# One core's decode attention beside an MLP: which engine issues the loads, and each load marked as one packet

## The chip, the core and the metric

The kernel runs on one of the eight cores of a Trainium2 chip. The core has TensorE (PE, matrix products), VectorE (DVE), ScalarE (ACT), GpSimd (POOL) and SyncE (SP), which work side by side and wait for one another by semaphores, and 16 DMA engines that move data between the memory (HBM) and the core's own SBUF. The metric is the time of one execution on the device in microseconds, as the median of several runs; shorter is better.

## The reference

One token's row `x` (512 numbers, bf16) goes through two branches, which a sigmoid gate mixes:

```python
g = sigmoid((x * gate_w).sum(-1))
q = (x @ wq).reshape(32 heads, 128)
a = concat_h(softmax(q_h @ k_cache_h.T * 128**-0.5) @ v_cache_h) @ wo
b = (silu(x @ w_gate) * (x @ w_up)) @ w_down
return g * a + (1 - g) * b
```

Each of the 32 heads has 65,536 cached keys and as many values of 128 numbers: 16.8 MB of K and as much V a head, some 1,074 MB in all. `wq` and `wo` are 4.2 MB each, `w_gate`, `w_up` and `w_down` 1.8 MB each. Every byte is used once.

## The kernel before

One SBUF tensor `mem` of 184 blocks of 1 KB per partition holds everything that is loaded. K and V of a head come in halves (`z` = 0 and 1), each 8.4 MB, 64 KB on each of the 128 partitions. K half 0 goes to block `KA` = 32, V half 0 to `VA` = 120 and V half 1 to `VZ` = 96; K half 1 goes to `KZ` = 0, except for head 0, where it goes to `V0` = 96, the place of `wq`. So the K halves of the next head may be loaded only when those of this one have been used, and likewise V.

**Start.** SyncE issues the weights (lines 211 to 213): `wq` to block 96, `w_gate` to 0, `w_up` to 14, `w_down` to 160. Then it issues K half 0 of head 0 in two pieces of 32 KB per partition, counted on `ka0` and `ka1` (225). ACT issues the rows `x` and `gate_w` (214, 215). PE computes q from `wq` (460, then `s_q`), lays it out (466), computes gate and up products (488), and with DVE's results in `guT` the down product (496, then `s_b`). GpSimd waits for `s_q` before it loads K half 1 of head 0 over `wq` (236, 237).

**A head.** DVE turns each K half by eight transposes of 32x32 blocks from `mem` into `kt` (lines 326 for head 0, 419 and 426 for the rest; `ktdone` counts them, 16 a head). PE takes each transposed piece and makes scores of it in the bank `psS` (476, `qkdone`). DVE then finds the maximum (340, 342), with PE's help for the step across partitions (551, 553); ACT takes the exponentials into `pa` (292); DVE shuffles them to `pb` (335); and PE multiplies them with V (529) in four parts, 40 and 24 matmuls for half 0 and 40 and 24 for half 1 (`pvdone` counts them, from 4). PE's values of a head run between the scores of the next: half 0 after six pieces of its first K half, half 1 after its second.

**Who issues what, and when.** From line 236 GpSimd issues all K and V, with a wait before each load for the place that it overwrites: K half 0 of head 1 at `ktdone` 8, V half 0 of head 0 at `ktdone` 13 and `s_b`, K half 1 of head 1 at `ktdone` 20, V half 1 of head 0 at `pvdone` 5; then a loop over the heads with the same four loads (247 to 255). At the end it issues `wo` without its last rows (257), the last head's V in eight pieces of falling size (`tail`, 264), and the rest of `wo` (266, 267). Each load has a semaphore that its landing raises by 16; K half 0 of heads 1 to 31 counts on `ka`, and line 411 waits for `16 i` in head `i`. ACT and SyncE store the result (306 and 228).

**End.** The last head's second half is multiplied piece by piece as the `tail` loads land (565), then mixed with the rest (604), copied (304) and stored.

Of the kernel before, what the change touches and what calls it, by code (L numbers as in the profile page):

```python
# [21 lines left out]
def bass_gated_mix__mha_block_cached__swiglu_ffn__decode_kernel(  # L22
# [11 lines left out]
    out: bass.AP,  # L34
):
    _, H, S, Dh = A_k_cache.shape
    D = A_wq.shape[0]
    F = B_w_gate.shape[1]
# [3 lines left out]
    HR = R // 2  # L42
# [6 lines left out]
    KA, KZ, VA, VZ, V0 = 32, 0, 120, 96, 96  # L49
# [13 lines left out]
    WOJ, WO31 = V0, V0 + 1  # L63

    with ExitStack() as ctx:
        def sb(name, shape, dt, align=32):
            return ctx.enter_context(nc.sbuf_tensor(name, shape, dt, align_bytes=align))
# [4 lines left out]
        def sem(name):  # L72
            return ctx.enter_context(nc.semaphore(name))
# [33 lines left out]
        fin = sb("fin", [P, 128], BF16)  # L107

        def at(kb, n):
            return mem[:, kb * KB:kb * KB + n]  # L110
# [7 lines left out]
        mrow, amx, Lt = psM[0:1, 0:128], psM[:, 256:257], psM[:, 257:258]  # L118
        gm = sc[0:1, 5:6]

        names = ("x", "gw", "wq", "wg", "wu", "wd", "ka0", "ka1", "ka", "kz", "va", "vz", "wo", "wj", "w31")
        d = {n: sem("d_" + n) for n in names}
        dt_ = [sem(f"d_t{i}") for i in range(len(tail))]
        s_ones = sem("s_ones")
# [50 lines left out]
        s_fin = sem("s_fin")  # L175
        s_zz = sem("s_zz")
        s_out2 = sem("s_out2")
# [3 lines left out]
        out_dram = out.rearrange("a b (c n) -> (a b c) n", c=4)  # L181
        gw_dram = gate_w.rearrange("(a d) -> a d", a=1)
        w_dram = {
            "wq": A_wq.rearrange("(p c) n -> p (c n)", c=Dc),
            "wg": B_w_gate.rearrange("(p c) f -> p (c f)", c=Dc),
            "wu": B_w_up.rearrange("(p c) f -> p (c f)", c=Dc),
            "wd": B_w_down.rearrange("(p c) n -> p (c n)", c=FC),
            "wo": A_wo.rearrange("(p j) n -> p (j n)", p=P),
        }
        wj_dram = w_dram["wo"][:, 31 * D:32 * D]  # L190
        w31_dram = A_wo.rearrange("(h d) n -> h d n", d=Dh)[H - 1]
        WQ, WG, WU, WD, WO = V0, 0, 14, V0 + 64, 64
# [8 lines left out]
        def place(kind, h, z):  # L201
            if kind == "k":
                return (KA, V0)[z] if isinstance(h, int) and h == 0 else (KA, KZ)[z]
            return (VA, VZ)[z]

        def kv_dram(cache, h):
            if isinstance(h, int):
                return cache[0, h].rearrange("(b p r) d -> b p (r d)", b=2, p=P)
            return cache[0, ds(h, 1)].rearrange("a (b p r) d -> b (a p) (r d)", b=2, p=P)

        for n, kb in (("wq", WQ), ("wg", WG), ("wu", WU), ("wd", WD)):
            src = w_dram[n]
            nc.sync.dma_start(at(kb, src.shape[1]), src).then_inc(d[n], 16)
        nc.scalar.dma_start(xrow[0:1, :], xr_dram).then_inc(d["x"], 16)
        nc.scalar.dma_start(gwrow[0:1, :], gw_dram).then_inc(d["gw"], 16)
        ctx.callback(lambda: nc.scalar.wait_ge(s_out, 16))
        ctx.callback(lambda: nc.sync.wait_ge(s_out2, 16))
        block = ctx.enter_context(nc.Block())

        half = HR // 2 * Dh  # L220

        @block.sync
        def _(sp):
            for n in range(2):
                sp.dma_start(at(KA + 32 * n, half), kv_dram(A_k_cache, 0)[0][:, n * half:n * half + half]).then_inc(
                    (d["ka0"], d["ka1"])[n], 16)
            sp.wait_ge(s_fin, 1)
            sp.dma_start(out_dram[2:4, :], fin[32:34, :]).then_inc(s_out2, 16)

        @block.gpsimd  # L230
        def _(pool):
            def load(kind, h, z):
                cache = A_k_cache if kind == "k" else A_v_cache
                pool.dma_start(at(place(kind, h, z), HR * Dh), kv_dram(cache, h)[z]).then_inc(d[kind + "az"[z]], 16)  # L234

            pool.wait_ge(s_q, 1)
            load("k", 0, 1)
            pool.wait_ge(ktdone, NP)
            load("k", 1, 0)
            pool.wait_ge(ktdone, 2 * NP - 3)  # L240
            pool.wait_ge(s_b, 1)
            load("v", 0, 0)
            pool.wait_ge(ktdone, 2 * NP + NP // 2)
            load("k", 1, 1)
            pool.wait_ge(pvdone, 5)
            load("v", 0, 1)
            with nc.gpsimd.Fori(0, H - 2) as i:  # L247
                pool.wait_ge(ktdone, i * (2 * NP) + (4 * NP - 4))
                load("k", i + 2, 0)
                pool.wait_ge(pvdone, i * 4 + 7)  # L250
                load("v", i + 1, 0)
                pool.wait_ge(ktdone, i * (2 * NP) + (4 * NP + NP // 2))  # L252
                load("k", i + 2, 1)
                pool.wait_ge(pvdone, i * 4 + 9)
                load("v", i + 1, 1)
            pool.wait_ge(ktdone, 2 * NP * H - NP)
            pool.dma_start(at(WO, 31 * D), w_dram["wo"][:, 0:31 * D]).then_inc(d["wo"], 16)
            src = A_v_cache[0, H - 1].rearrange("(b p r) d -> b p (r d)", b=2, p=P)
            need = {0: (ktdone, 2 * NP * H - 4), 1: (ktdone, 2 * NP * H), 2: (pvdone, 4 * H - 1)}
            for n, (kb, r0, nr) in enumerate(tail):  # L260
                if n in need:
                    pool.wait_ge(*need[n])
                b, o = divmod(r0, HR)
                pool.dma_start(at(kb, nr * Dh), src[b][:, o * Dh:(o + nr) * Dh]).then_inc(dt_[n], 16)  # L264
            pool.wait_ge(pvdone, 4 * H)
            pool.dma_start(at(WOJ, D), wj_dram).then_inc(d["wj"], 16)
            pool.dma_start(at(WO31, D), w31_dram).then_inc(d["w31"], 16)

        @block.scalar
        def _(act):  # L270
# [38 lines left out]
        def _(dve):  # L309
# [7 lines left out]
            def transposes(z):  # L317
                dve.wait_ge(d[("ka0", "kz")[z]], 16)
                for c, u in enumerate(k_order[z]):
                    i = NP * z + c  # L320
                    if i == NP // 2:
                        dve.wait_ge(d["ka1"], 16)
                    if i >= 2:
                        dve.wait_ge(qkdone, i - 1)
                    src = at(place("k", 0, z) + 8 * u, PR * Dh).bitcast(U32)
                    nc.vector.transpose(kt[:, i % 2, :].rearrange("p (j r t) -> p r j t", j=2, t=32),  # L326
                                        src.rearrange("p (r j t) -> p r j t", j=2, t=32)).then_inc(ktdone, 1)

            def shuffle(z, s):
                c0 = 256 * z  # L330
                for g in range(4):
                    for b in range(4):
                        dst = pb[32 * g:32 * g + 32, c0:c0 + 256].rearrange("p (n b) -> p n b", b=4)[:, :, b]
                        sr = pa[32 * b:32 * b + 32, c0:c0 + 256].rearrange("p (n g) -> p n g", g=4)[:, :, g]
                        last = nc.vector.tensor_copy(dst, sr)  # L335
                last.then_inc(s, 1)
# [7 lines left out]
            def late(pv, sl, so):  # L344
                dve.wait_ge(pvdone, pv)
                shuffle(1, s_pbz)
                dve.wait_ge(s_L, sl)
                dve.wait_ge(s_or, so)
                nc.vector.reciprocal(Li, Lt).then_inc(s_li, 1)
# [57 lines left out]
            with nc.vector.Fori(1, H) as i:  # L407
                n = i * (2 * NP)
                v = i * 4
                dma = i * 16  # L410
                dve.wait_ge(d["ka"], dma)
                for c, u in enumerate(k_order[0]):
                    if c == NP // 2:
                        dve.wait_ge(expdone, i)
                        dve.wait_ge(pvdone, v - 2)
                        shuffle(0, s_pba)
                    dve.wait_ge(qkdone, n + (c - 1))  # L417
                    src = at(KA + 8 * u, PR * Dh).bitcast(U32)
                    nc.vector.transpose(kt[:, c % 2, :].rearrange("p (j r t) -> p r j t", j=2, t=32),  # L419
                                        src.rearrange("p (r j t) -> p r j t", j=2, t=32)).then_inc(ktdone, 1)  # L420
                late(v, i, i)
                dve.wait_ge(d["kz"], dma + 16)
                for c, u in enumerate(k_order[1]):
                    dve.wait_ge(qkdone, n + (NP + c - 1))
                    src = at(KZ + 8 * u, PR * Dh).bitcast(U32)
                    nc.vector.transpose(kt[:, c % 2, :].rearrange("p (j r t) -> p r j t", j=2, t=32),  # L426
                                        src.rearrange("p (r j t) -> p r j t", j=2, t=32)).then_inc(ktdone, 1)
                top(i, n + 2 * NP)
# [206 lines left out]
```

## Time and profile before

| | |
|---|---|
| median of 3 runs | 2527.52 us (2527.16 to 2527.83) |
| profiled execution, its time | 2528.12 us |
| its span, first to last instruction | 2526.7 us |
| busy: PE, DVE, ACT, POOL | 1708.3, 1412.3, 64.7, 73.3 us |
| moved by DMA | 1087.93 MB, 431 GB/s over the span |
| queue 0 (GpSimd's loads) | 19,232 packets, 1069.69 MB |
| queue 1 (SyncE's) | 868 packets, 18.09 MB |
| granted TensorE clock, mean | 0.722 |

The view of DMA issues gives for each kind of load its median time from issue to landing: 29.1 us for the three V tail loads of 4 MB, 12.3 for `wq`, 16.0, 23.3 and 44.3 for the three MLP weights, 58.0 for the two K pieces that SyncE issues.

How to read it: "busy" adds up an engine's own instructions. A row of a timeline gives start, length, engine, source line, operation, output and input; in brackets stand the idle time before it and what ended it. The engine name with a q (SPq, POOLq) is its sequencer, which issues DMAs. In a row of windows stand the stretch, its length, the busy time of PE, PEld (weight loading), DVE, ACT and POOL with the number of instructions, the granted clock, the mean share in which the 16 DMA engines were busy, and GB/s. A row of a DMA queue gives its kind, packets, MB and the time of its packets as a share of the 16 engines' time in the stretch. A row of DMA issues gives tile and source, the issuer, how many, KB of each where that is known, and the median us from issue to landing.

### The profile page before, as it was taken

Reading aid. Unit: us, or ns where it says so; the run is one execution under the profiler, and the core shown is the slowest. Engines: PE = TensorE matmul, PEld = TensorE weight load, DVE = VectorE, ACT = ScalarE, POOL = GpSimd, SP = SyncE. Lnnn points to the kernel's source line nnn. Section 1 sums busy time; section 2 is a strip of 40 time slices with the busy share of each in tenths; the row PEclk is TensorE's granted clock in tenths of the full one; section 3 lists DMA queues with packets and bytes.
Section 4 is the critical chain, followed back from the end, with each engine's and each line's share of the span. In section 5 each row is a group of like instructions: output and inputs, shape, how many; then the busy total and the mean of one; then the engine's idle time right before and its main releaser. Section 6 shows DMA issues by size and latency. Waiting matters only on the chain.

```text
span 2526.7 us, 51725 instructions
## 1 busy us (share of the span) xinstructions
PE 1708.3 (68%) x21624; PEld 978.0 (39%) x21624; DVE 1412.3 (56%) x1683; ACT 64.7 (3%) x195; POOL 73.3 (3%) x140
## 2 busy tenths in 40 slices
PE   3567676676676676666776766766667767677677
PEld 2434333343333343333343334433333433344334
DVE  2854655645646446555466464565554664645653
ACT  0000000000000000000000000000000000000000
POOL 0000000000000000000000000000000000000000
PEclk9577677676776776776767767767767677677677
DMA  9899999999999999999999999999999999999999
GB/s 419 348 433 431 433 433 432 432 444 434 433 433 432 432 441 437 432 434 432 432 440 438 432 433 433 432 432 442 436 433 433 432 432 441 437 432 434 432 432 402
DMA packets 20119, 1087.93 MB, mean 431 GB/s; under 512 B 2283, under 2 KB 2285, under 8 KB 2573
## 3 DMA queue, kind: packets, MB, share of 16 engines
q0 software_dynamic: 19232, 1069.69, 97.7%
q1 hardware_dynamic: 868, 18.09, 1.7%
q8 instruction: 9, 0.15, 0.0%
q14 instruction: 2, 0.01, 0.0%
q10 hardware_dynamic: 8, 0.00, 0.0%
HBM read 1087.77 MB, written 0.00 MB: 431 GB/s over the span
## 4 chain that ended last, share of the span: by engine, by line
DMA 68%; PE 27%; issue 5%; POOLq 0%; DVE 0%; POOL 0%; ACT 0%; DVEq 0%
DMA mem<-in_A_v_cache_dram 67%; PE psO L529 26%; DMA mem<-in_A_k_cache_dram 1%; DMA mem<-in_A_wq_dram 0%; DVE kt L419 0%; POOLq L234 0%; PE psM L460 0%; POOL mem L264 0%; POOL mem L234 0%; PE psZ L604 0%; POOLq L247 0%; POOLq L252 0%; PE psW L565 0%; ACT fin L304 0%; DVEq L417 0%
## 5 line engine op out<-in xcount | busy, mean ns | idle before, releaser
L476 PE MATMUL psS<-qcur,kt 128*128 128x4 bf16 x16384 | 572.0, 169 | 726.9 <-DVE kt L419 416.6
L529 PE MATMUL psO<-mem,pb 128*4 128x512 bf16 x3968 | 1040.3, 428 | 33.1 <-DMA mem<-in_A_v_cache_dram 33.1
L476 PEld LDWEIGHTS psS<-qcur,kt 128*128 128x128 bf16 x16384 | 533.0, 105 | 790.2 <-issue 787.9
L426 DVE STREAM_TRANSPOSE kt<-mem 128x2048 uint32<-128x2048 uint32 x248 | 547.6, 2275 | 405.2 <-DMA mem<-in_A_k_cache_dram 405.2
L419 DVE STREAM_TRANSPOSE kt<-mem 128x2048 uint32<-128x2048 uint32 x248 | 551.2, 2280 | 241.7 <-DMA mem<-in_A_k_cache_dram 240.7
L529 PEld LDWEIGHTS psO<-mem,pb 128*4 128x4 bf16 x3968 | 359.4, 93 | 657.5 <-issue 237.7
L335 DVE COPY pb<-pa 32x64 bf16<-32x64 bf16 x1024 | 234.1, 229 | 15.0 <-ACT pa L292 1.5
L342 DVE TENSOR_REDUCE sc<-psM 1x1 f32<-1x128 f32 x32 | 8.9, 279 | 333.4 <-PE psM L551 333.4
L234 POOL DMA_DIRECT2D mem<-in_A_v_cache_dram x62 | 32.8, 529 | 1274.3 <-PE psO L529 1263.9
L234 POOL DMA_DIRECT2D mem<-in_A_k_cache_dram x63 | 34.4, 546 | 1106.2 <-DVE kt L419 525.0
L326 DVE STREAM_TRANSPOSE kt<-mem 128x2048 uint32<-128x2048 uint32 x16 | 35.3, 2274 | 23.5 <-DMA mem<-in_A_k_cache_dram 23.5
L340 DVE TENSOR_REDUCE sm<-psS 128x1 f32<-128x512 f32 x32 | 22.1, 692 | 42.2 <-PE psS L476 42.2
L290 ACT ACTIVATE sm<-psM 128x1 f32<-128x1 f32 x32 | 5.5, 171 | 1231.6 <-PE psM L553 1231.6
L286 ACT ACTIVATE oTn<-psT,gcol 128x1 f32 (+1 forms) x31 | 8.2, 264 | 1035.9 <-PE psT L503 1035.9
L503 PE MATMUL psT<-ident,orow 4*128 4x1 f32 x256 | 33.5, 248 | 0.5 <-ACT orow L284 0.5
L503 PEld LDWEIGHTS psT<-ident,orow 4*128 4x128 f32 x256 | 30.8, 186 | 1.2 <-ACT orow L284 0.6
L284 ACT ACTIVATE orow<-psO,sm 4x512 f32<-4x512 f32 x31 | 21.0, 678 | 130.3 <-PE psO L529 125.9
L292 ACT ACTIVATE pa<-psS,sm 128x512 bf16<-128x512 f32 x32 | 22.0, 687 | 1.0
L553 PE MATMUL psM<-sc,onesf 1*128 1x1 f32 x64 | 12.3, 259 | 11.9 <-DVE sc L342 11.9
L565 PE MATMUL psW<-pb,mem 128*128 128x1 bf16 x512 | 14.6, 165 | 6.9 <-DMA mem<-in_A_v_cache_dram 6.4
L553 PEld LDWEIGHTS psM<-sc,onesf 1*128 1x128 f32 x64 | 9.6, 186 | 21.5 <-DVE sc L342 21.5
L565 PEld LDWEIGHTS psW<-pb,mem 128*128 128x128 bf16 x512 | 14.0, 102 | 8.1 <-issue 5.9
(78 smaller groups left out, 121.6 us busy)
## 6 DMA issues: line engine op xcount, KB each, us to landing
mem<-in_A_v_cache_dram POOLq DMA_DIRECT2D x3, 4096.0 KB, 29.1
mem<-in_A_k_cache_dram SPq DMA_DIRECT2D x2, 4096.0 KB, 58.0
mem<-in_A_wq_dram SPq DMA_DIRECT2D x1, 4096.0 KB, 12.3
mem<-in_A_wo_dram POOLq DMA_DIRECT2D x1, 3968.0 KB, 36.1
mem<-in_A_v_cache_dram POOLq DMA_DIRECT2D x1, 2048.0 KB, 32.9
mem<-in_B_w_gate_dram SPq DMA_DIRECT2D x1, 1792.0 KB, 16.0
mem<-in_B_w_up_dram SPq DMA_DIRECT2D x1, 1792.0 KB, 23.3
mem<-in_B_w_down_dram SPq DMA_DIRECT2D x1, 1792.0 KB, 44.3
```

The costliest lines, as they stand in the source:

```text
L234: pool.dma_start(at(place(kind, h, z), HR * Dh), kv_dram(cache, h)[z]).then_inc(d[kind + "az"[z]], 16)
L292: nc.scalar.activation(pa[:], psS[:], ACT.Exp, bias=nbias, scale=SCALE, accum_out=rsum).then_inc(expdone, 1)
L326: nc.vector.transpose(kt[:, i % 2, :].rearrange("p (j r t) -> p r j t", j=2, t=32), src.rearrange("p (r j t) -> p r j t", j=2, t=32)).then ...
L335: last = nc.vector.tensor_copy(dst, sr)
L340: nc.vector.reduce_max(mxs, psS[:], AX_X).then_inc(s_mx, 1)
L419: nc.vector.transpose(kt[:, c % 2, :].rearrange("p (j r t) -> p r j t", j=2, t=32), src.rearrange("p (r j t) -> p r j t", j=2, t=32)).then ...
L426: nc.vector.transpose(kt[:, c % 2, :].rearrange("p (j r t) -> p r j t", j=2, t=32), src.rearrange("p (r j t) -> p r j t", j=2, t=32)).then ...
L476: last = nc.tensor.matmul(psS[:, o:o + 4] if j is None else psS[:, ds(j * (2 * PR) + o, 4)], ktb[b][:, je // 2, r, :, je % 2], qcur[:, je, ...
L503: last = nc.tensor.matmul(psT[:, 0:1], orow[0:4, i * Dh:(i + 1) * Dh], ident[0:4, i:i + 1], start=(i == 0), stop=(i == 3))
L529: last = nc.tensor.matmul(psO[0:4, :], pb[:, k_col[256 * z + r]:k_col[256 * z + r] + 4], vt[:, r * Dh:(r + 4) * Dh], start=(z == 0 and par ...
L553: nc.tensor.matmul(amx, onesf[0:1, :], gm, start=True, stop=True).then_inc(s_ar, 1)
L565: last = nc.tensor.matmul(psW[:, 0:1], vt[:, r * Dh:(r + 1) * Dh], pb[:, col:col + 1], start=(r0 + r == 0), stop=(r0 + r == R - 1))
```

## The change

All loads of weights, K and V are issued by GpSimd. The four weight loads stand there ahead of the two pieces of K half 0 of head 0, these ahead of the wait for `s_q` and the loads that GpSimd had before, whose order and waits are the same. Each of GpSimd's loads carries `single_packet=True`, which marks it to go as one packet per DMA engine. The second K piece counts on `ka` in place of `ka1`, so that DVE's waits on `ka` are 16 higher. SyncE keeps the last store.

```diff
-        names = ("x", "gw", "wq", "wg", "wu", "wd", "ka0", "ka1", "ka", "kz", "va", "vz", "wo", "wj", "w31")
+        names = ("x", "gw", "wq", "wg", "wu", "wd", "ka0", "ka", "kz", "va", "vz", "wo", "wj", "w31")
...
-            nc.sync.dma_start(at(kb, src.shape[1]), src).then_inc(d[n], 16)
+            nc.gpsimd.dma_start(at(kb, src.shape[1]), src, single_packet=True).then_inc(d[n], 16)
...
-        @block.sync
-        def _(sp):
-            for n in range(2):
-                sp.dma_start(at(KA + 32 * n, half), kv_dram(A_k_cache, 0)[0][:, n * half:n * half + half]).then_inc(
-                    (d["ka0"], d["ka1"])[n], 16)
-            sp.wait_ge(s_fin, 1)
-            sp.dma_start(out_dram[2:4, :], fin[32:34, :]).then_inc(s_out2, 16)
-
         @block.gpsimd
         def _(pool):
             def load(kind, h, z):
                 cache = A_k_cache if kind == "k" else A_v_cache
-                pool.dma_start(at(place(kind, h, z), HR * Dh), kv_dram(cache, h)[z]).then_inc(d[kind + "az"[z]], 16)
+                pool.dma_start(at(place(kind, h, z), HR * Dh), kv_dram(cache, h)[z], single_packet=True).then_inc(d[kind + "az"[z]], 16)
+
+            half = HR // 2 * Dh
+            for n in range(2):
+                pool.dma_start(at(KA + 32 * n, half), kv_dram(A_k_cache, 0)[0][:, n * half:n * half + half], single_packet=True).then_inc(
+                    (d["ka0"], d["ka"])[n], 16)
             pool.wait_ge(s_q, 1)
             load("k", 0, 1)
...
-            pool.dma_start(at(WO, 31 * D), w_dram["wo"][:, 0:31 * D]).then_inc(d["wo"], 16)
+            pool.dma_start(at(WO, 31 * D), w_dram["wo"][:, 0:31 * D], single_packet=True).then_inc(d["wo"], 16)
...
-                pool.dma_start(at(kb, nr * Dh), src[b][:, o * Dh:(o + nr) * Dh]).then_inc(dt_[n], 16)
+                pool.dma_start(at(kb, nr * Dh), src[b][:, o * Dh:(o + nr) * Dh], single_packet=True).then_inc(dt_[n], 16)
             pool.wait_ge(pvdone, 4 * H)
-            pool.dma_start(at(WOJ, D), wj_dram).then_inc(d["wj"], 16)
-            pool.dma_start(at(WO31, D), w31_dram).then_inc(d["w31"], 16)
+            pool.dma_start(at(WOJ, D), wj_dram, single_packet=True).then_inc(d["wj"], 16)
+            pool.dma_start(at(WO31, D), w31_dram, single_packet=True).then_inc(d["w31"], 16)
+
+        @block.sync
+        def _(sp):
+            sp.wait_ge(s_fin, 1)
+            sp.dma_start(out_dram[2:4, :], fin[32:34, :]).then_inc(s_out2, 16)
...
-                        dve.wait_ge(d["ka1"], 16)
+                        dve.wait_ge(d["ka"], 16)
...
-                dve.wait_ge(d["ka"], dma)
+                dve.wait_ge(d["ka"], dma + 16)
```

More of the change, by code (lines that the diff above doesn't have):

```diff
@@ L218, in bass_gated_mix__mha_block_cached__swiglu_ffn__decode_kernel @@
         block = ctx.enter_context(nc.Block())
-        half = HR // 2 * Dh
-        @block.sync
-        def _(sp):
-            for n in range(2):
-                sp.dma_start(at(KA + 32 * n, half), kv_dram(A_k_cache, 0)[0][:, n * half:n * half + half]).then_inc(
-                    (d["ka0"], d["ka1"])[n], 16)
-            sp.wait_ge(s_fin, 1)
-            sp.dma_start(out_dram[2:4, :], fin[32:34, :]).then_inc(s_out2, 16)
         @block.gpsimd
```

## The prediction

> **What bounds the kernel now.** I read the page first: what each engine does over the span, the DMA rows, the chain, and the costliest rows.
>
> ```profile
> span 2526.7 us, 51725 instructions
> PE 1708.3 (68%) x21624; PEld 978.0 (39%) x21624; DVE 1412.3 (56%) x1683; ACT 64.7 (3%) x195; POOL 73.3 (3%) x140
> ...
> DMA  9899999999999999999999999999999999999999
> GB/s 419 348 433 431 433 433 432 432 444 434 433 433 432 432 441 437 432 434 432 432 440 438 432 433 433 432 432 442 436 433 433 432 432 441 437 432 434 432 432 402
> DMA packets 20119, 1087.93 MB, mean 431 GB/s; under 512 B 2283, under 2 KB 2285, under 8 KB 2573
> ...
> q8 instruction: 9, 0.15, 0.0%
> ```
>
> The transfers are the bound: the DMA digit is 9 almost everywhere and 1087.93 MB leave at 431 GB/s, while PE is busy for 68% and DVE for 56%. The three slices below 430 are the first, the second (348) and the last. Slice 2 (63 to 126 us) lacks 85 of 433 GB/s, 12.4 us of traffic. So I cut the beginning into stretches (the view of windows; last columns: clock, DMA share, GB/s) and set a long steady stretch beside them.
>
> ```profile
> 0.00:1.90 1.90, 0.00 (x0) 0.00 (x0) 0.78 (x3) 0.20 (x1) 0.20 (x4) 1.00 0.06 18
> 1.90:12.50 10.60, 0.26 (x4) 0.21 (x4) 6.55 (x30) 1.28 (x2) 0.00 (x0) 1.00 0.99 401
> ...
> 44.00:65.60 21.60, 9.12 (x119) 5.12 (x120) 8.89 (x4) 0.00 (x0) 0.00 (x0) 0.74 0.91 394
> 65.60:76.30 10.70, 5.19 (x156) 4.77 (x152) 10.39 (x5) 0.00 (x0) 0.54 (x1) 0.50 0.01 2
> ...
> 200.00:2450.00 2250.00, 1549.68 (x19069) 873.83 (x19068) 1269.76 (x1485) 57.63 (x175) 63.34 (x118) 0.72 1.00 434
> ```
>
> From 65.6 to 76.3 us nothing is transferred: 10.7 us. Elsewhere the engines run at 434 GB/s with share 1.00, so a hole at the start is never made up and stands whole in the end. The timeline tells where it comes from.
>
> ```profile
> 0.87 0.40 SPq L213 DMA_DIRECT2D mem<-in_A_wq_dram  x1
> 2.85 0.95 SPq L225 DMA_DIRECT2D mem<-in_A_k_cache_dram  x2
> ...
> 13.26 3.55 PE L460 MATMUL psM<-xTb,mem 128*128 128x1 bf16 x128 [10.72 <-DMA mem<-in_A_wq_dram]
> 17.13 0.67 POOL L234 DMA_DIRECT2D mem<-in_A_k_cache_dram  x1 [16.55 <-PE psM L460]
> 25.25 6.86 PE L488 MATMUL psM<-xTb,mem 128*128 128x1 bf16 x112 [7.34 <-DMA mem<-in_B_w_up_dram]
> 32.14 0.18 ACT L278 ACTIVATE hbuf<-psM 128x14 f32<-128x14 f32 x1 [12.62 <-PE psM L488]
> ...
> 33.25 0.23 DVE L403 TENSOR_SCALAR guT<-hbuf,gcol 128x14 bf16<-128x14 f32 x1
> 46.63 5.27 PE L496 MATMUL psY<-mem,guT 128*1 128x512 bf16 x14 [14.53 <-DMA mem<-in_B_w_down_dram]
> 56.27 8.89 DVE L326 STREAM_TRANSPOSE kt<-mem 128x2048 uint32<-128x2048 uint32 x4 [22.78 <-DMA mem<-in_A_k_cache_dram]
> 65.91 26.44 DVE L326 STREAM_TRANSPOSE kt<-mem 128x2048 uint32<-128x2048 uint32 x12 [0.76 <-DMA mem<-in_A_k_cache_dram]
> 75.12 0.54 POOL L234 DMA_DIRECT2D mem<-in_A_k_cache_dram  x1 [57.32 <-DVE kt L326]
> ...
> 95.06 0.28 DVE L342 TENSOR_REDUCE sc<-psM 1x1 f32<-1x128 f32 x1 [0.68 <-PE psM L551]
> ...
> 98.14 8.89 DVE L419 STREAM_TRANSPOSE kt<-mem 128x2048 uint32<-128x2048 uint32 x4 [2.81 <-DMA mem<-in_A_k_cache_dram]
> ...
> 117.68 11.19 PE L529 MATMUL psO<-mem,pb 128*4 128x512 bf16 x40 [1.01 <-DMA mem<-in_A_v_cache_dram]
> ```
>
> SyncE issued the K half of head 0 (two pieces, ka0 and ka1) at 2.85; its first piece is used at 56.27. GpSimd's load at 17.13, the other half (kz), is issued 14 us later but passes it, though nobody can use kz before ka is transposed. The queues between 21.2 and 44 us show that:
>
> ```profile
> q0 software_dynamic: 125, 8.19, 83.0%
> q1 hardware_dynamic: 123, 1.65, 16.9%
> ```
>
> GpSimd's queue took 83% of the engines, SyncE's 17%, with nearly as many packets each (125 and 123): the engines take one packet of one queue and one of the other, and a packet of kz is larger (8.19 MB / 125, 65.5 KB) than one of the weights (1.65 MB / 123, 13.4 KB). So ka is late, its eight transposes end at 75, only then may K of head 1 go into its place (75.12), and by 65.6 all else had landed.
>
> **The change, part by part.** *Six loads move from SyncE to GpSimd.* On one queue in order of issue, kz comes last. Up to 76.3 us the kernel moved 26.5 MB (weights 9.70, ka0 and ka1 4.19 each, kz 8.39). At 434 GB/s that is 61.1 us, so 15.2 us were lost: 1.9 before the first packet, 10.7 in the hole, 2.6 in slower stretches. The changed kernel keeps the 1.9, and of the 2.6 what the first stretch shows (401 against 434 GB/s over 10.6 us, 0.8 us); I allow 1.2, since the ragged end (394 GB/s) only arises where nothing follows. To this comes what GpSimd's first issue is slower than SyncE's. SyncE took 1.0 us from issue (0.87) to traffic (1.9). The queues between 17.2 and 21 us, just after GpSimd's first load was issued, are these:
>
> ```profile
> q1 hardware_dynamic: 115, 1.58, 97.6%
> q8 instruction: 1, 0.02, 1.6%
> ```
>
> Queue 0 is not among them, so that load took 3.9 us (17.13 to 21) to its traffic; the next took 1.2 (75.12 to 76.3). So 0.2 to 2.9 us more; below nothing only the barrier's tenths could reach. I take 1.5, between them, as the first load is a first one too but meets no traffic. The other five issues at 0.53 to 0.67 us are over by about 5, before wq has landed, and hide behind its 9.7 us.
>
> So kz ends at 1.9 + 1.5 + 1.2 + 61.1 = 65.7 where K of head 1 could begin at 76.3: a gain of 10.6 us, if that load is in the queue by 65.7. Cumulated bytes at 434 GB/s on 4.6 us, plus 0.4 to land: wu 23.1, wd 27.4, ka0 37.0, ka1 46.7. PE: L488 from 23.1 to 30.0, the hbuf steps (32.14 to 33.48 in the rows above) to 31.3, L496 to 36.6, so PE is ready for ka0. DVE transposes 37.0 to 45.9 and 46.7 to 55.6; then K of head 1 is issued, 10 us before the queue ends. Thirteen transposes are done at 66.1 + 5 x 2.22 = 77.2, which releases the V load; the queue then lasts to 85. The next K load follows after head 0's reductions (3.0 us from the last transpose's end at 92.35 to 95.34) and four transposes, at about 96, against 104. For the values of head 0, the page's row gives the mean of one matmul (428 ns):
>
> ```profile
> L529 PE MATMUL psO<-mem,pb 128*4 128x512 bf16 x3968 | 1040.3, 428 | 33.1 <-DMA mem<-in_A_v_cache_dram 33.1
> ```
>
> Forty of them (L529) take 17.1 us so, and 11.2 in the timeline's row; from 105, that issues the next V load at 116 to 122, against 124. Each load is in time by 2 to 10 us, so no new hole.
>
> After that everything is shifted as a whole, because loads are issued early all along, as the view of DMA issues shows (last column: us from issue to landing; the last row is of the stretch from 65.6 to 76.3):
>
> ```profile
> mem<-in_A_k_cache_dram POOLq DMA_DIRECT2D x63, 29.0
> mem<-in_A_v_cache_dram POOLq DMA_DIRECT2D x62, 27.0
> ...
> mem<-in_A_k_cache_dram POOLq DMA_DIRECT2D x1, 22.9
> ```
>
> A V load takes 27.0 us and a K load 29.0, but 22.9 the one that found the queue empty: 4 to 6 us are spent queued.
>
> *SyncE only stores; ka1 counts on semaphore ka.* The store waits for the last ACT copy as before, and the waits on ka are 16 higher for 16 more counts: nothing.
>
> *One packet for each engine.* The steady stretch and a tail stretch of 16 KB packets (2513.5 to 2516.7 us) give the time of a packet by size:
>
> ```profile
> DMA packets 16766, 977.15 MB, mean 434 GB/s; under 512 B 1856, under 2 KB 1856, under 8 KB 1856
> q0 software_dynamic: 16766, 977.15, 100.2%
> ...
> DMA packets 84, 1.36 MB, mean 425 GB/s; under 512 B 1, under 2 KB 1, under 8 KB 1
> q0 software_dynamic: 84, 1.36, 99.1%
> ```
>
> 16,766 less 1,856 small ones are 14,910 packets of 65,536 B, eight per engine and load (1,856 / 16 = 116 loads): 1.002 x 2250 x 16 / 14,910 = 2.419 us. The 83 of 16,384 B take 0.991 x 3.2 x 16 / 83 = 0.611, four of them 2.445. The 0.026 us are three times what a packet costs beside its bytes, 9 ns. With 17,836 packets (20,119 less 2,283), 1,115 per engine, that is 10 us; if one packet in place of eight saves seven eighths, 8.8 us. At the other end, each load could lose what the empty queue's load shows beyond its bytes (22.9 less 19.3, 3.6 us), times 130 loads: 470 us, far off. I take nothing, nearest to the row of 434 GB/s, where packets already follow without a gap.
>
> The Trainium skill, "DMA: Bandwidth & Descriptors", section "Why small descriptors are slow (HBM only)", names a fixed overhead per packet that joining descriptors removes, and says that this is only worth it at descriptors of 256 B or less. By that rule the gain of 8.8 would be nothing and the sum stays; by the 9 ns, which is 0.4% of a packet, it could all come.
>
> *Sum.* 2526.7 - 10.6 = 2516.1 of span. The profiled execution took 2528.12, 1.4 over its span, and the median (2527.52) is 0.6 under that: 2516.9 us.
>
> **Rivals.** *The packets' 9 ns go as well:* 2516.9 - 8.8 = 2508. For it: the size of the packet term. Against: nothing shows that it belongs to the packet's end rather than to each address.
>
> *The queue doesn't keep the order, or GpSimd starts much later:* the hole stays, plus 1.5 us: 2529. Against it: late loads on queue 0 land in turn today.
>
> *One packet holds an engine for 8 x 2.419 = 19.4 us, and instruction fetches wait behind it.* The row of queue 8 after 2490 us:
>
> ```profile
> q8 instruction: 4, 0.07, 0.6%
> ```
>
> That is four of its nine pieces of 16 KB; none falls from 200 to 2450, where queue 0 is alone, so five come at the start, while PE runs its loop for the first time. If PE needs three of them behind half a packet each (9.7, less the 4 us that loads are early), the cost is 17 us: 2534, slower. It decides from 10.6 us of uncovered waiting on. Against it: no row shows PE waiting for code, and the loop comes round without fetching. The Trainium skill, same page, section "Queues, rings and completion order", says that an engine drains a whole packet of one ring before it turns to the next; the 125 against 123 packets agree.
>
> *Each load ends with a gap,* as the end of one long packet: 0.08 us for each of some 130 loads eats the gain, a tenth of a 2.42 us packet gives 2516.9 + 31 = 2548. No row speaks for it.
>
> **How the numbers follow.** Forecast 0.50, packets' time gone 0.22, hole stays 0.10, fetches 0.10, gaps 0.08. A measurement of this kernel tells about 0.2% (5 us) from no change. Faster 0.50 + 0.22 = 0.72; same 0.10 (2529 is within 5 us); slower 0.18. The range goes down to 2516.9 - 8.8 - 2.6 = 2505.5, 2506, with all packet time and pace regained, and up to 2527, a start that gives back nearly all its gain; what is left out is the slower 0.18 and little else.
>
> **What would show it.** Right: GpSimd's second K load stands at 53 to 59 us, not 75; the stretch from 65.6 to 76.3 shows over 400 GB/s; ka0 is transposed from about 37; the steady stretch stays at 434 GB/s, and 11 us are missing in front. Wrong in the packet term: the steady 2250 us move more or less than 977 MB. Wrong in the start: SyncE's old 1.9 us of silence grows past 5, or a hole opens ahead of a V load because PE stands still between 66 and 105 us. What would overturn the forecast altogether is a steady rate below 431 GB/s.

## The result, and the profile after

| | before | after |
|---|---|---|
| median of the runs | 2527.52 us (2527.16 to 2527.83) | 2514.91 us (2514.62 to 2515.72) |
| ratio, 95% interval | | 0.9951 [0.9936, 0.9965] |
| span of the profiled execution | 2526.7 us | 2513.3 us |

Forecast were 2516.9 us; measured are 2.0 less. The gain is half a per cent, 12.6 us between the medians, and the interval of the ratio lies below 1. One of the four executions of the kernel without the mark, below, took 2831.45 us at a granted clock of 0.588 and stays out of its ratio. The page of the changed kernel: the DMA digits and rates in 40 slices, then the queue of the loads (packets, MB, share of the 16 engines).

```profile
span 2513.3 us, 51694 instructions
...
DMA  9999999999999999999999999999999999999999
GB/s 418 432 434 434 434 434 434 434 434 434 435 434 434 434 434 434 434 434 434 435 435 434 434 434 436 434 434 435 434 434 434 434 434 434 434 434 434 434 434 404
...
q0 software_dynamic: 20096, 1087.78, 99.9%
```

The second slice stands at 432 GB/s, where 348 stood before, and queue 0 carries nearly everything (1087.78 of 1087.93 MB). The same stretches as before, from the view of windows (last: clock, DMA share, GB/s):

```profile
1.90:2.70 0.80, 0.26 (x4) 0.20 (x4) 0.64 (x7) 0.80 (x1) 0.80 (x3) 1.00 0.01 1
2.70:12.50 9.80, 0.00 (x0) 0.00 (x0) 5.82 (x24) 0.48 (x2) 1.94 (x4) 1.00 1.05 428
...
44.00:65.60 21.60, 6.75 (x192) 6.26 (x192) 11.56 (x6) 0.00 (x0) 0.53 (x1) 0.50 1.05 452
65.60:76.30 10.70, 3.82 (x107) 3.59 (x108) 9.37 (x5) 0.00 (x0) 0.00 (x0) 0.50 0.96 416
...
200.00:2450.00 2250.00, 1545.58 (x19043) 872.16 (x19042) 1275.24 (x1483) 57.46 (x174) 62.70 (x117) 0.72 1.00 434
```

The stretch from 65.6 to 76.3 us carries 416 GB/s where it carried 2, and the long stretch stands at 434 as before. The silence at the start has grown: traffic begins after 2.7 us, where it began after 1.9. (A row of windows counts each packet, with all its time and bytes, in the stretch in which it starts; that is how a share can pass 1.00.) The timeline of the start:

```profile
1.37 0.67 POOL L213 DMA_DIRECT2D mem<-in_A_wq_dram  x1 [0.80 <-POOLq L619]
...
14.07 3.55 PE L459 MATMUL psM<-xTb,mem 128*128 128x1 bf16 x128 [11.55 <-DMA mem<-in_A_wq_dram]
...
37.78 8.89 DVE L325 STREAM_TRANSPOSE kt<-mem 128x2048 uint32<-128x2048 uint32 x4 [5.55 <-DMA mem<-in_A_k_cache_dram]
47.45 8.89 DVE L325 STREAM_TRANSPOSE kt<-mem 128x2048 uint32<-128x2048 uint32 x4 [0.77 <-DMA mem<-in_A_k_cache_dram]
56.63 0.53 POOL L224 DMA_DIRECT2D mem<-in_A_k_cache_dram  x1 [38.18 <-DVE kt L325]
66.93 17.66 DVE L325 STREAM_TRANSPOSE kt<-mem 128x2048 uint32<-128x2048 uint32 x8 [10.59 <-DMA mem<-in_A_k_cache_dram]
78.31 0.53 POOL L224 DMA_DIRECT2D mem<-in_A_v_cache_dram  x1 [21.15 <-DVE kt L325]
96.80 0.53 POOL L224 DMA_DIRECT2D mem<-in_A_k_cache_dram  x1 [17.97 <-DVE kt L418]
117.28 0.53 POOL L224 DMA_DIRECT2D mem<-in_A_v_cache_dram  x1 [19.95 <-PE psO L528]
```

The loads are now used in the order in which they are issued. The first weights are used 0.8 us later than before (14.07 against 13.26), ka 18.5 us earlier (37.78 against 56.27), and so is K half 0 of head 1 issued (56.63 against 75.12), 10 us before kz is used (66.93).

### The profile page after: what moved, and what is told of

It reads as the page before. It is cut to its first block, busy times and chain, and to the rows that moved or that the text cites. A ratio compares the mean times of both kernels' runs of the same rounds, so it can differ in the third digit from the quotient of the medians.

```text
span 2513.3 us, 51694 instructions
## 1 busy us (share of the span) xinstructions
PE 1709.4 (68%) x21624; PEld 978.5 (39%) x21624; DVE 1412.1 (56%) x1683; ACT 64.6 (3%) x195; POOL 76.3 (3%) x146
## 2 busy tenths in 40 slices
DMA packets 20118, 1087.93 MB, mean 433 GB/s; under 512 B 2282, under 2 KB 2284, under 8 KB 2572
## 3 DMA queue, kind: packets, MB, share of 16 engines
q0 software_dynamic: 20096, 1087.78, 99.9%
## 4 chain that ended last, share of the span: by engine, by line
DMA 69%; PE 27%; issue 3%; DVE 1%; POOLq 0%; POOL 0%; ACT 0%; DVEq 0%
DMA mem<-in_A_v_cache_dram 67%; PE psO L528 26%; DMA mem<-in_A_k_cache_dram 2%; DVE kt L325 1%; DMA mem<-in_A_wq_dram 1%; DVE kt L418 0%; POOLq L224 0%; PE psM L459 0%; POOL mem L258 0%; PE psS L475 0%; DVE sm L339 0%; PE psZ L603 0%; POOLq L241 0%; POOLq L246 0%; PE psM L550 0%
## 5 line engine op out<-in xcount | busy, mean ns | idle before, releaser
L552 PE MATMUL psM<-sc,onesf 1*128 1x1 f32 x64 | 12.3, 259 | 11.9 <-DVE sc L341 11.9
## 6 DMA issues: line engine op xcount, KB each, us to landing
mem<-in_A_wq_dram POOLq DMA_DIRECT2D x1, 4096.0 KB, 12.6
mem<-in_B_w_gate_dram POOLq DMA_DIRECT2D x1, 1792.0 KB, 16.1
```

The lines of the kernel that those rows point to most:

```text
L552: nc.tensor.matmul(amx, onesf[0:1, :], gm, start=True, stop=True).then_inc(s_ar, 1)
```

## The experiments

Two questions were open: does the gain come from the order on one queue or from the one-packet mark, and why is it larger than the 10.6 us that were priced? "Order theory" says that kz no longer passes ka and that this is all; "mark theory" gives the mark a share. All ratios below are against the kernel before.

**One queue without the mark.** Every `single_packet=True` is taken out of the changed kernel.

```diff
-pool.dma_start(..., single_packet=True)
+pool.dma_start(...)
```

> All loads on GpSimd's queue, without the one-packet mark. Order theory (the whole gain comes from kz no longer passing ka): 2514.9 us as in the changed kernel, within 1.5; K half 0 of head 1 issued at 56 to 57 us; steady stretch 434 GB/s. Mark theory (the mark carries the 2.8 us of gain beyond the predicted 10.6, or more): 2517.5 to 2522 us.

Measured: 2514.9 us, ratio 0.995 [0.993, 0.997], the time of the changed kernel. The second K load of its timeline:

```profile
56.66 0.53 POOL L224 DMA_DIRECT2D mem<-in_A_k_cache_dram  x1 [38.05 <-DVE kt L325]
```

It stands at 56.66, with the mark at 56.63. The mark has no part in the gain that shows.

**The mark without the one queue.** The kernel before, with the mark on GpSimd's loads.

```diff
-pool.dma_start(at(place(kind, h, z), HR * Dh), kv_dram(cache, h)[z])
+pool.dma_start(at(place(kind, h, z), HR * Dh), kv_dram(cache, h)[z], single_packet=True)
```

> The kernel before, with the mark on GpSimd's loads alone; SyncE's loads are as before. Order theory, where the mark changes nothing between queues: 2527.5 us within 1.5, kz still has some 83% of the engines between 21 and 44 us and lands near 46, ka0 is used at 56. Rival, where a marked load is one packet that the engine finishes before it turns to the other queue: queue 0 has over 95% while kz runs, kz is through by 42 us, SyncE's queue stands still for some 19 us, ka0 still near 56; time 2527 to 2530. Mark theory on the rate: 2519 to 2524 us.

Measured: 2527.5 us, ratio 0.9999 [0.999, 1.0009]. Its queues from 21.2 to 44 us:

```profile
q0 software_dynamic: 125, 8.19, 83.0%
q1 hardware_dynamic: 120, 1.63, 16.7%
```

Queue 0 has 83.0% as without the mark, and the packets of the two queues still alternate one for one. The counts say so, and so does the order: where the next packet of an engine can be told by its start within 6 ns of the end of the last, it belongs to the other queue in 167 of 172 cases before and in 185 of 188 with the mark. A marked load doesn't hold an engine for its eight pieces, so the rival with the fetches behind a packet of 19.4 us has no ground either.

**Only the overtaking undone.** The kernel before; GpSimd holds kz until ka has landed.

```diff
             pool.wait_ge(s_q, 1)
+            pool.wait_ge(d["ka1"], 16)
             load("k", 0, 1)
```

> The kernel before, with GpSimd waiting for ka1 to land before it issues kz; SyncE still issues the weights and ka, nothing is marked. Order theory: ka0 is used at 36 to 38 us, kz is issued at about 46 and starts after a gap of 1.2 to 3.9 us, no hole from 65.6 to 76.3; 2515 to 2518 us. Rival, where the gain needs one queue or the mark: 2524 us or more.

Measured: 2519.05 us, ratio 0.9967 [0.9954, 0.9979], so two thirds of the gain with the engines as before, but 1 us outside what was expected. Its timeline and its windows around the change of queues:

```profile
37.21 8.89 DVE L327 STREAM_TRANSPOSE kt<-mem 128x2048 uint32<-128x2048 uint32 x4 [5.89 <-DMA mem<-in_A_k_cache_dram]
...
47.45 0.67 POOL L234 DMA_DIRECT2D mem<-in_A_k_cache_dram  x1 [46.88 <-DMA mem<-in_A_k_cache_dram]
```

```profile
44.00:46.50 2.50, 1.48 (x40) 1.40 (x41) 2.10 (x1) 0.00 (x0) 0.00 (x0) 0.50 0.09 39
46.50:48.80 2.30, 0.90 (x29) 0.82 (x27) 1.94 (x1) 0.00 (x0) 0.67 (x1) 0.50 0.00 0
```

The gap without traffic is 2.3 us, inside the 1.2 to 3.9. But few packets start in the 2.5 us before it (a share of 9%): most engines finish their part of ka early and wait for the last ones, since nothing is queued behind. The row overstates that, as packets that started before 44 us still run in it. With the bytes of each packet in the trace spread evenly over its duration, this uneven end costs 1.7 us. The uneven start after the gap costs another 0.9 by 52 us, against the steady 434 GB/s. So the hole costs 2.3 + 1.7 + 0.9 = 4.9 us, and less what SyncE's earlier first packet saves (0.8, below) that is 4.1, as between this median and the changed kernel's. This is the first sight of the larger price of a hole.

**SyncE as the one issuer.** The changed kernel's order, all on SyncE.

```diff
-nc.gpsimd.dma_start(at(kb, src.shape[1]), src, single_packet=True)
+nc.sync.dma_start(at(kb, src.shape[1]), src)
...
-        @block.gpsimd
+        @block.sync
```

> The changed kernel's order with SyncE as the issuer of every load, nothing marked. Order theory: the same as the changed kernel less its later first packet (0.8 us at the first 4 MB): 2514 us, 2513 to 2516. Rival, where SyncE's queue is slower for loads that are issued late, or its issue stalls: 2520 us or more.

Measured: 2513.93 us (2513.79 to 2514.07), ratio 0.9946 [0.9929, 0.9962]. It is the lowest median of all kernels here, 1.0 us under the changed one, though the two intervals overlap. Its timeline:

```profile
0.74 0.41 SPq L213 DMA_DIRECT2D mem<-in_A_wq_dram  x1
...
66.08 17.66 DVE L322 STREAM_TRANSPOSE kt<-mem 128x2048 uint32<-128x2048 uint32 x8 [10.41 <-DMA mem<-in_A_k_cache_dram]
```

SyncE issues at 0.74 where GpSimd did at 1.37, and kz is there at 66.08 and not 66.93, 0.85 us sooner. Of this, 0.13 is an earlier start of the whole program (ACT's first issue, too, stands at 0.74 here and at 0.87 in the changed kernel). With one queue, it matters little whose it is.

**A late load, to make a hole.** The changed kernel issues K half 0 of head 1 five transposes later.

```diff
-            pool.wait_ge(ktdone, NP)
+            pool.wait_ge(ktdone, 2 * NP - 3)
             load("k", 1, 0)
```

> The changed kernel, but K half 0 of head 1 is issued at ktdone 13 in place of 8, together with the V load behind it: a hole of our own making. It would be issued at about 78 us with the queue empty from 65.9 on, so 13.6 us without traffic. If a hole costs its own length and about 2.8 us more for engines that end and start unevenly (the 2.8 by which the prediction fell short): 2514.9 + 16.4 = 2531 us, 2530 to 2532.5. If a hole costs its length alone: 2528.5 us. If loads issued later catch it up: under 2525 us.

Measured: 2530.76 us, ratio 1.0013 [1.0003, 1.0022], and 15.9 us over the changed kernel (2514.91), as the larger price said. Its windows:

```profile
61.60:64.00 2.40, 0.00 (x0) 0.00 (x0) 0.00 (x0) 0.00 (x0) 0.00 (x0) 0.50 1.01 437
64.00:66.70 2.70, 0.00 (x0) 0.00 (x0) 0.00 (x0) 0.00 (x0) 0.00 (x0) 0.50 0.08 30
66.70:79.60 12.90, 5.93 (x160) 5.50 (x160) 12.58 (x6) 0.00 (x0) 1.05 (x2) 0.50 0.00 0
```

The hole has 12.9 us without traffic. With the packets' bytes spread over their durations, the uneven end ahead of it (64.0 to 66.7) costs 1.5 us, and the uneven start behind it 0.9 by 84 us. That makes 15.3; the 0.6 left over is not accounted for.

**kz on SyncE, the rest on GpSimd.** The mirror image of the kernel before, with the mark on GpSimd's loads.

```diff
-            pool.wait_ge(s_q, 1)
-            load("k", 0, 1)
...
+            sp.wait_ge(s_q, 1)
+            sp.dma_start(at(place("k", 0, 1), HR * Dh), kv_dram(A_k_cache, 0)[1]).then_inc(d["kz0"], 16)
```

> The changed kernel with kz alone moved to SyncE, which waits for s_q and issues it on its own queue; GpSimd has all the rest, in the same order. Order theory: the mirror of the kernel before, two queues again, kz passes ka, ka0 is used at 54 to 58 us, a hole before K half 0 of head 1; 2527 to 2530 us. Rival, where it is GpSimd's queue as such that passes SyncE's: ka0 is used at 37 to 40 us and the time stays at 2515 to 2518 us.

Measured: 2528.26 us, ratio 1.0003 [0.9993, 1.0012]. Queues from 21.2 to 44 us, and the load after the hole:

```profile
q1 hardware_dynamic: 127, 8.32, 84.2%
q0 software_dynamic: 126, 1.58, 16.3%
```

```profile
75.91 0.53 POOL L224 DMA_DIRECT2D mem<-in_A_k_cache_dram  x1 [71.26 <-DVE kt L325]
```

The shares are swapped, packets alternate again (127 and 126), and the whole gain is gone. Neither engine's queue goes first by itself: the one with the larger packets gets the larger share.

**kz in small packets.** The kernel before, with nothing else touched.

```diff
-            load("k", 0, 1)
+            pool.dma_start(at(V0, HR * Dh), kv_dram(A_k_cache, 0)[1], max_dma_last_dim=4096).then_inc(d["kz"], 16)
```

> The kernel before, engines, order and queues untouched, but kz goes in packets of 8 KB in place of 64 KB. If engines alternate packet by packet between the queues, kz gets 36% beside the weights' 14 KB and 20% beside ka's 32 KB: ka1 is through near 52 us, its eighth transpose ends near 62, K half 0 of head 1 is issued before the queues end at 65.5, no hole: 2514 to 2517 us. If the share goes by bytes or by queue and not by packets: 2526 us or more.

Measured: 2514.84 us, ratio 0.9949 [0.9933, 0.9966]: the full gain, with both queues, both issuers and the early kz of before. The queues from 21.2 to 44 us and the timeline:

```profile
q1 hardware_dynamic: 362, 8.46, 86.1%
q0 software_dynamic: 339, 1.39, 14.9%
```

```profile
39.91 8.89 DVE L326 STREAM_TRANSPOSE kt<-mem 128x2048 uint32<-128x2048 uint32 x4 [8.62 <-DMA mem<-in_A_k_cache_dram]
...
60.16 0.55 POOL L234 DMA_DIRECT2D mem<-in_A_k_cache_dram  x1 [41.65 <-DVE kt L326]
```

The packets came out at 4 KB (1.39 MB / 339) and not the 8 KB of the expectation, so kz had 14.9%, and the second piece of ka was there at 50.96, sooner still than the 52 expected. Again the packets' numbers are nearly equal, and again the share follows their size.

**Smaller packets all along, with and without the mark.** The changed kernel with GpSimd's loads of a whole K or V half in smaller packets, then the same with no load marked.

```diff
-kv_dram(cache, h)[z], single_packet=True)
+kv_dram(cache, h)[z], max_dma_last_dim=8192, single_packet=True)
```

> The changed kernel with K and V in packets of 16 KB, marked. If the mark does nothing, each quarter of 64 KB costs the 9 ns of a packet of its own: 1048 MB / 16 / 65,536 B = 1000 packets times 27 ns, 27 us more: 2541 to 2543 us. If the mark makes one packet of an engine's 32 pieces, most of it is saved: 2515 to 2519 us.

> The run before (K and V in packets of 16 KB) without the mark. If the mark does nothing at this size either: 2547.6 us as with it, within 1.5. If it saves part of a packet's cost: 2550 us or more.

Measured: 2547.64 us (ratio 1.0079 [1.0059, 1.01]) with the mark and 2547.55 (1.0079 [1.0049, 1.0108]) without: the mark does nothing at this size either. The steady stretch from 200 to 2450 us of the marked one, beside the changed kernel's:

```profile
DMA packets 119496, 963.85 MB, mean 428 GB/s; under 512 B 1840, under 2 KB 1840, under 8 KB 1840
q0 software_dynamic: 119496, 963.85, 101.0%
```

```profile
DMA packets 16782, 977.21 MB, mean 434 GB/s; under 512 B 1871, under 2 KB 1871, under 8 KB 1871
```

The packets were 8 KB (963.85 MB over 119,496 less 1,840), not 16, so there were seven more in each 64 KB and not three: the time lies above the expected 2541 to 2543, though each packet cost less than assumed. Per 64 KB an engine took 2250 x 16 / (963.85 / 0.065536) = 2.448 us against 2.414, 0.033 more for seven more packets: 4.8 ns each on average. That is about half of the 9 ns by which the prediction bounded the mark's gain.

## Why the prediction was right, and where it was off

*The bound and the cause.* A hole in the traffic stands whole in the end: shown by the late load of K, whose hole cost 15.9 us and was not made up in the 2400 us that followed. The hole came from kz passing ka by packets of larger size: shown three ways, by holding kz back, by swapping the issuers and by making kz's packets small. The mechanism was forecast, and it is what happened.

*The chain of the start.* Every step came within 1.3 us of its place: ka0 at 37.78 (37.0), the second piece at 47.45 (46.7), K of head 1 at 56.63 (55.6), V at 78.31 (77.2), the next K at 96.80 (96), the next V at 117.28 (116 to 122). No new hole arose. Nearly all came 0.7 to 1.1 us late, although GpSimd started sooner than priced: the 0.4 us for landing was too small. As many bytes as end with kz had been moved by 64.9 us, but kz was used at 66.93, when the last engine was done.

*GpSimd's first issue.* Priced at 1.5 us more than SyncE's, in bounds of 0.2 to 2.9; it was 0.8. The first weights are used 0.81 later than before (14.07 against 13.26): 0.50 of this is later issue (1.37 against 0.87), the rest lies on the way to traffic. This accounts for 0.7 of the missing gain.

*The restart after the hole.* This is a term that the sum left out. How far each kernel lies behind a steady 434.3 GB/s (977.21 MB in 2250 us) can be worked out from the packets of the two traces, with the bytes of each spread evenly over its duration:

| us behind, at | 8 us | 63 us | 65.6 us | 76.3 us | 84 us |
|---|---|---|---|---|---|
| before | 2.8 | 3.0 | 4.4 | 15.1 | 16.1 |
| after | 3.6 | 3.9 | 4.0 | 4.0 | 4.0 |

Up to 76.3 us the prediction has it right: 15.1 lost (15.2 in its own sum), of which 1.4 is the uneven end of the traffic just ahead of the hole, as much as the prediction let go. But 1.0 more is lost between 76.3 and 84, when traffic sets in again. In the trace, the first sixteen packets of 64 KB start over 1.3 us (76.36 to 77.67) and take 2.9 us on average, where 2.42 is usual. This loss went with the hole. The account is now 10.7 + 1.4 + 1.0 - 0.8 = 12.3 us, where 12.6 were measured between the medians; the 0.3 left over is less than the executions of one kernel differ by (0.7 and 1.1 us).

The row of windows just ahead of the hole, of the kernel before, invites a larger figure for the uneven end:

```profile
63.00:65.60 2.60, 1.51 (x41) 1.44 (x42) 2.16 (x1) 0.00 (x0) 0.00 (x0) 0.50 0.12 50
```

A share of 12% over 2.6 us looks like 2.3 us lost. But only the packets that start in it are counted, and packets of 32 KB that started before 63 us ran on for up to 1.2 us. The loss is 1.4.

*The mark.* Taken as nothing, and nothing of it shows, with and without a second queue and at two packet sizes: the medians with and without it differ by 0.1 us at most. The steady stretch moved 977.21 MB against 977.15. The rival with 8.8 us more did not come: its 9 ns were about twice the 4.8 that the rate shows, and the mark doesn't join packets in any way that the trace shows.

*The rule on small descriptors.* The Trainium skill, "DMA: Bandwidth & Descriptors", section "Why small descriptors are slow (HBM only)", holds joining to be worth it at 256 B or less. The runs agree as far as they go: at 64 KB and 8 KB the mark gave nothing. No run here had loads in pieces of 256 B.

*The rule on whole packets.* The Trainium skill, same page, section "Queues, rings and completion order", has an engine drain a packet of several descriptors before it turns to the next ring. Here the turns go by single pieces of 4 to 64 KB, marked or not (339 against 362, 125 against 120), and the measurement decides. So the 125 against 123, which the prediction took for agreement, agree only if a packet holds a single piece; the eight pieces that a load of 8.4 MB gives each engine are not drained in one go.

## What to carry to other kernels

Where a kernel is bound by transfers, look for the slices of low rate and follow each to the load that was issued late; then ask what delayed the wait behind it. A load that is needed later should not run on another queue beside one that is needed sooner, unless its packets are smaller: here packets alternated, so the share went by their size. The cure can be one queue, whoever issues on it, or one argument that sets the packet size. A hole costs more than its silence: the uneven end ahead of it and the uneven start behind it, 2.4 to 2.6 us together here, are part of its price. And know how a view counts before its share becomes a term of a sum.

## What had not been expected of the hardware

Packet durations can add up to more than the engines' time: 101.0% of the stretch with 8 KB packets, where it was 100.2% with 64 KB. So a packet's duration overstates what it costs; the rate showed 4.8 ns a packet where durations had suggested 9. And traffic that sets in again after a hole does so slowly: in the three traces with a hole worked out above, the first sixteen packets of 64 KB took 2.9 to 3.2 us on average, where 2.42 is usual.
